# First loads in one line on SyncE, and the first block in halves: a SwiGLU feed-forward kernel on Trainium2

## The chip, the cores and the metric

The kernel runs on one core of one Trainium2 chip. The metric is the device time of one execution in microseconds, the median of several runs. Before the change it is 163.57 us (three runs, 163.53 to 163.64).

## The reference

The program computes a SwiGLU feed-forward layer on 2048 rows of 640 values, with 1536 hidden channels, all in bf16:

```python
# x (1, 2048, 640), w_gate (640, 1536), w_up (640, 1536), w_down (1536, 640)
def reference(x, w_gate, w_up, w_down):
    g = _silu(x @ w_gate)
    u = x @ w_up
    return (g * u) @ w_down
```

## The kernel before

The 2048 rows are worked in four blocks of 512 (`S_BLK`), the 1536 hidden channels in twelve f chunks of 128, and the 640 input channels in five slices of 128, which the code calls kd. For each block and each f chunk, five matmuls (one for each kd) build the gate product in a PSUM tile `pg`, and five the up product in `pu`; weights are the stationary operand, 128 x 128, and the transposed input `xT` streams 512 columns past it. ScalarE applies Silu to `pg` (L214), VectorE multiplies the result with `pu` and writes `aT` (L215). After the twelve chunks of a block, the down projection follows on TensorE: twelve matmuls into `po_t` (L261) and 48 into `po_a` (L291), which ScalarE copies out and SyncE stores.

The last four rows are computed on VectorE instead, by dot products that run beside the matmuls of the later blocks (L147); they and the late transfers for them are not touched by the change.

**How the input gets its transposed form.** The matmuls need x with its channels on the partitions. For rows 0 to 255 (`HALF`), two chunks of 128 rows are loaded as they are (L86) and turned on TensorE, five transposes each (L185); ScalarE copies the first two slices of each chunk to `xT`, VectorE the other three (L190). For all other rows the transfer engines turn the data themselves, in a crossbar copy (a transposing DMA, L105); the one for rows 256 to 511 is the first of them.

**The order of the front.** The instructions of an engine run in the order in which they are written, and a transfer is issued by an engine's queue in that order too. SyncE issues: x chunk 0, the gate slices of kd 0, 2, 3, 4 for f chunks 0 to 3 (`EARLY`, L115, 128 KB each), the crossbar copy of rows 256 to 511, the up weights of f chunks 0 to 3 in two loads (L83, 320 KB each), and then gate and up weights of chunks 4 to 7 and of chunks 8 to 11 (`W_CHUNKS`, 640 KB each), the down weights (1920 KB), and the rest. ScalarE issues x chunk 1 and the gate slice of kd 1, then loads its function table and runs a first Silu (L119). Eight semaphores serve the transfers in turn, so a load waits at its issue for the one eight before it.

TensorE starts with 18 matmuls on a constant tile (`warm`, L176, `N_WARM`), whose result is not used. Then come the ten transposes, and in `head()` the gate products of f chunks 0 to 3 together, kd by kd: kd 0 in two parts of 128 columns, kd 1 to 4 on 256 columns (the first half of the block), then all five on the second half, which needs the crossbar copy. These four `pg` tiles stay open at the same time. Then the up products of the four chunks follow on 512 columns each, and Silu and multiply for each. From f chunk 4 on the regular loop runs (L245 on), with 512 columns in every matmul. PSUM has four buffers of the tag `gu` and two each of `po_a` and `po_b`; the up tiles of the head use the latter two.

Of the kernel before, what the change touches and what calls it, by code (L numbers as in the profile page):

```python
# [10 lines left out]
def _body(  # L11
# [8 lines left out]
    nc = tc.nc  # L20
    P = nc.NUM_PARTITIONS
    f32 = mybir.dt.float32
    bf16 = mybir.dt.bfloat16
    ACT = mybir.ActivationFunctionType
    ALU = mybir.AluOpType
# [7 lines left out]
    KD = D // P  # L33
    KF = F // P
    S_BLK = 512
    NSB = S // S_BLK
    SUB = S_BLK // P
    HALF = S_BLK // 2
    DA = 512
    Q = 32  # L40
    N_WARM = 18
    T = 4
    WT_STEP = 4
    ROW_J = 0
    EARLY = 4
    W_CHUNKS = [(4, 8), (8, 12)]
    assert D % P == 0 and F % P == 0 and S % S_BLK == 0 and D > DA and SUB == 4

    consts = ctx.enter_context(tc.tile_pool(name="consts", bufs=1))
# [2 lines left out]
    psum = ctx.enter_context(  # L52
        tc.tile_pool(name="psum", bufs=2, space=bass.MemoryType.PSUM)
    )
# [3 lines left out]
    xT = consts.tile([P, KD, S], bf16)  # L58
    wg_sb = consts.tile([P, KD, F], bf16)
    wu_sb = consts.tile([P, KD, F], bf16)  # L60
    wd_sb = consts.tile([P, KF, D], bf16)
    aT = consts.tile([P, KF, S], bf16)
# [12 lines left out]
    wg_v = w_gate.rearrange("(kd p) f -> p kd f", p=P)  # L75
    wu_v = w_up.rearrange("(kd p) f -> p kd f", p=P)
    wd_v = w_down.rearrange("(kf p) d -> p kf d", p=P)

    def wslice(a, b):
        return slice(a * P, b * P)  # L80

    def load_w(eng, dst, src, a, b):
        eng.dma_start(out=dst[:, :, wslice(a, b)], in_=src[:, :, wslice(a, b)])  # L83

    def load_x(eng, c0, c1):
        eng.dma_start(out=x_sb[:, c0:c1, :], in_=x_v[:, c0:c1, :])  # L86
# [20 lines left out]
    ones = consts.tile([P, P], bf16)  # L107
    silu_first = consts.tile([P, 1], f32)
    nc.vector.memset(ones[:], 1.0)  # L109

    load_x(nc.sync, 0, 1)
    load_x(nc.scalar, 1, 2)
    for kd in range(KD):
        eng = nc.scalar if kd == 1 else nc.sync
        eng.dma_start(  # L115
            out=wg_sb[:, kd, wslice(0, EARLY)], in_=wg_v[:, kd, wslice(0, EARLY)]
        )
    turn_x(HALF, S_BLK)
    nc.scalar.activation(silu_first[:], ones[:, 0:1], ACT.Silu)  # L119
    for a in range(0, EARLY, 2):  # L120
        load_w(nc.sync, wu_sb, wu_v, a, a + 2)
    for a, b in W_CHUNKS:
        load_w(nc.sync, wg_sb, wg_v, a, b)
        load_w(nc.sync, wu_sb, wu_v, a, b)
# [4 lines left out]
    def turn_w(dst, src, f0, f1):  # L129
# [7 lines left out]
        out=x_row[:],  # L137
        in_=x2[S - T : S, :].rearrange("t d -> (t d)").partition_broadcast(P),
# [35 lines left out]
    def warm(n):  # L174
        for _ in range(n):
            nc.tensor.matmul(  # L176
                pw[:, 0:P], lhsT=ones[:], rhs=ones[:], start=True, stop=True
            )

    def transpose_chunk(c, parts):  # L180
        c_sl = slice(c * P, (c + 1) * P)
        for copy, tag, k0, k1 in parts:
            pt = psum.tile([P, k1 - k0, P], bf16, tag=tag, name="pt")
            for kd in range(k0, k1):
                nc.tensor.transpose(  # L185
                    out=pt[:, kd - k0, :],
                    in_=x_sb[:, c, kd * P : (kd + 1) * P],
                    identity=ident[:],
                )
            copy(out=xT[:, k0:k1, c_sl], in_=pt[:])  # L190

    def proj_step(ps, w_sb, fc, sb, c0, c1, kd):
        nc.tensor.matmul(  # L193
            ps[:, c0:c1],
            lhsT=w_sb[:, kd, fc * P : (fc + 1) * P],
            rhs=xT[:, kd, sb * S_BLK + c0 : sb * S_BLK + c1],
            start=(kd == 0 and c0 in (0, HALF)),
            stop=(kd == KD - 1),
        )

    def proj(ps, w_sb, fc, sb, c0, c1):
        for kd in range(KD):
            proj_step(ps, w_sb, fc, sb, c0, c1, kd)

    def gu_tiles():
        pg = psum.tile([P, S_BLK], f32, tag="gu", name="pg", bufs=4)
        pu = psum.tile([P, S_BLK], f32, tag="gu", name="pu", bufs=4)
        return pg, pu

    def gate(pg, pu, sb, fc, n_s):  # L210

        s0 = sb * S_BLK
        sg = work.tile([P, S_BLK], f32, name="sg")
        nc.scalar.activation(sg[:, 0:n_s], pg[:, 0:n_s], ACT.Silu)  # L214
        nc.vector.tensor_tensor(  # L215
            out=aT[:, fc, s0 : s0 + n_s], in0=sg[:, 0:n_s], in1=pu[:, 0:n_s], op=ALU.mult
        )

    def head():
        dve, act = nc.vector.tensor_copy, nc.scalar.copy  # L220
        split = [(act, "po_a", 0, 2), (dve, "po_b", 2, KD)]
        pgs = [
            psum.tile([P, S_BLK], f32, tag="gu", name="pg", bufs=4)
            for _ in range(EARLY)
        ]
        warm(N_WARM)
        for c in range(HALF // P):
            transpose_chunk(c, split)

        steps = [(0, 0, P), (0, P, HALF)]  # L230
        steps += [(kd, 0, HALF) for kd in range(1, KD)]
        steps += [(kd, HALF, S_BLK) for kd in range(KD)]
        for kd, c0, c1 in steps:
            for fc in range(EARLY):
                proj_step(pgs[fc], wg_sb, fc, 0, c0, c1, kd)

        for fc in range(EARLY):
            pu = psum.tile([P, S_BLK], f32, tag=("po_a", "po_b")[fc % 2], name="pu")
            proj(pu, wu_sb, fc, 0, 0, S_BLK)
            gate(pgs[fc], pu, 0, fc, S_BLK)  # L240
        keep_order(mybir.EngineType.PE)
        keep_order(mybir.EngineType.Activation)

    head()
    for sb in range(NSB):  # L245
        n_s = S_BLK if sb < NSB - 1 else S_BLK - T
        for fc in range(KF):
            if sb == 0 and fc < EARLY:
                continue
            pg, pu = gu_tiles()  # L250
            proj(pg, wg_sb, fc, sb, 0, n_s)
            proj(pu, wu_sb, fc, sb, 0, n_s)
            gate(pg, pu, sb, fc, n_s)
            if sb > 0 and fc < KF - 2:
                do_dots(2)


        n_t = (SUB if sb < NSB - 1 else SUB - 1) * P
        po_t = psum.tile([P, n_t], f32, tag="po_b", name="po_t")
        for kf in range(KF):  # L260
            nc.tensor.matmul(  # L261
                po_t[:],
                lhsT=wd_sb[:, kf, DA:D],
                rhs=aT[:, kf, sb * S_BLK : sb * S_BLK + n_t],
                start=(kf == 0),
                stop=(kf == KF - 1),
            )
        ot_t = outp.tile([P, n_t], bf16, name="ot_t")
        ot_q = outp.tile([P, n_t], bf16, name="ot_q")
        nc.scalar.copy(ot_t[:], po_t[:])  # L270
        do_dots(3)
        nc.vector.transpose(out=ot_q[:], in_=ot_t[:])  # L272
        for q in range(P // Q):
            nc.scalar.dma_start(
                out=out2[
                    sb * S_BLK : sb * S_BLK + n_t, DA + q * Q : DA + (q + 1) * Q
                ].rearrange("(i r) c -> r i c", r=Q),
                in_=ot_q[q * Q : (q + 1) * Q, :].rearrange("r (i c) -> r i c", c=Q),
            )
# [141 lines left out]
```

## Time and profile before

| what | value |
|---|---|
| median of 3 runs | 163.57 us (163.53 to 163.64) |
| profiled execution, first to last instruction | 161.8 us |
| TensorE busy | 159.4 us, 808 matmuls |
| VectorE busy | 111.0 us |
| ScalarE busy | 42.6 us |
| bytes moved by the transfer engines | 15.86 MB |
| granted TensorE clock, mean | 1.000 |

The profiled execution is told by its span, 161.8 us from the first to the last instruction; the time of a run is measured around it and is some 1.8 us longer. Its own time is not listed beside the span, so the runs' median stands for it. All start times in the profile count from the first instruction. A matmul's busy time includes the time until its result has drained, which overlaps the next matmul; what a matmul costs in a row of them is the distance from start to start.

### The profile page before, as it was taken

The page shows a single profiled execution, that of the slowest core. Times are in us where ns is not written, and L with a number is a line of the kernel's source. Part 1 is how long each engine was busy: PE and PEld are TensorE (multiplying, and loading weights), DVE is VectorE, ACT ScalarE, POOL GpSimd, SP SyncE. Part 2 cuts the span into 40 slices and gives each one's busy share as a digit, 9 for nine tenths or more (in the row PEclk, how much of TensorE's full clock was granted, in tenths as well). Part 3 has the DMA queues.
Part 4 walks back from the last instruction along what each step waited for, and adds up shares of the span by engine and source line. Part 5 has one row for each costly group of instructions (what it writes and reads, how often), then busy time and mean ns, then how long its engine had stood idle before and what let it go on. Part 6 is the DMA issues. An engine that isn't in the chain of part 4 may idle for free.

```text
span 161.8 us, 2142 instructions
## 1 busy us (share of the span) xinstructions
PE 159.4 (99%) x808; PEld 77.6 (48%) x808; DVE 111.0 (69%) x250; ACT 42.6 (26%) x74; POOL 0.6 (0%) x6
## 2 busy tenths in 40 slices
PE   8999999999999999999999999999999999999995
PEld 7854444444444444444444444444444444445454
DVE  2034223599569999989919999979964999993001
ACT  5051222112222222211222322221214222222121
POOL 1000000000000000000000000000000000000000
PEclk9999999999999999999999999999999999999999
DMA  6999999934189999003110000000321000000312
GB/s 212 231 351 349 361 248 231 222 75 91 34 192 159 235 236 184 4 0 34 65 65 0 0 4 2 0 0 3 62 67 34 0 0 0 0 0 4 48 41 73
DMA packets 41961, 15.86 MB, mean 98 GB/s; under 512 B 33504, under 2 KB 41824, under 8 KB 41952
## 3 DMA queue, kind: packets, MB, share of 16 engines
q1 hardware_dynamic: 33584, 14.93, 37.0%
q10 hardware_dynamic: 8368, 0.80, 3.5%
q8 instruction: 6, 0.10, 0.3%
q14 instruction: 3, 0.02, 0.1%
HBM read 6.88 MB, written 2.62 MB: 59 GB/s over the span
## 4 chain that ended last, share of the span: by engine, by line
PE 97%; DMA 2%; SPq 0%; DVE 0%; issue 0%
PE pg L193 32%; PE pu L193 32%; PE po_a L291 26%; PE po_t L261 6%; DMA wg_sb<-in_w_gate_dram 2%; SPq L86 0%; DVE ot_b L302 0%
## 5 line engine op out<-in xcount | busy, mean ns | idle before, releaser
L193 PE MATMUL pg<-xT,wg_sb 128*128 128x512 bf16 (+3 forms) x264 | 59.8, 363 | 0.1
L193 PE MATMUL pu<-xT,wu_sb 128*128 128x512 bf16 (+1 forms) x240 | 59.1, 379 | 0.0
L215 DVE TENSOR_TENSOR aT<-sg,pu 128x512 bf16<-128x512 f32 (+1 forms) x48 | 32.7, 682 | 32.3 <-PE pu L193 32.3
L214 ACT ACTIVATE sg<-pg 128x512 f32<-128x512 f32 (+1 forms) x48 | 28.4, 597 | 71.2 <-PE pg L193 67.4
L291 PE MATMUL po_a<-wd_sb,aT 128*128 128x512 bf16 (+4 forms) x228 | 42.8, 348 | 0.0
L147 DVE SCALAR_TENSOR_TENSOR prod<-wgT,x_row 128x640 f32<-128x640 bf16 x48 | 39.4, 821 | 1.5 <-DMA wgT<-in_w_gate_dram 0.4
L147 DVE SCALAR_TENSOR_TENSOR prod<-wuT,x_row 128x640 f32<-128x640 bf16 x48 | 39.4, 821 | 1.0
L193 PEld LDWEIGHTS <-wg_sb 128*128 128x128 bf16 x264 | 25.9, 100 | 26.8 <-DMA wg_sb<-in_w_gate_dram 0.4
L193 PEld LDWEIGHTS <-wu_sb 128*128 128x128 bf16 x240 | 23.4, 98 | 28.1 <-DMA wu_sb<-in_w_up_dram 0.3
L291 PEld LDWEIGHTS <-aT 128*128 128x128 bf16 x228 | 20.8, 98 | 21.7
L300 ACT CAST ot<-po_a 128x512 bf16<-128x512 f32 (+2 forms) x17 | 9.5, 559 | 31.8 <-PE po_a L291 20.2
L261 PE MATMUL po_t<-aT,wd_sb 128*128 128x512 bf16 (+1 forms) x48 | 10.4, 366 | 0.0
L261 PEld LDWEIGHTS <-wd_sb 128*128 128x128 bf16 x48 | 4.7, 98 | 5.1
L302 DVE CAST ot_b<-po_a 128x96 bf16<-128x96 f32 (+1 forms) x2 | 0.5, 240 | 9.7 <-PE po_a L291 9.6
L270 ACT CAST ot_t<-po_t 128x512 bf16<-128x512 f32 (+1 forms) x4 | 2.2, 559 | 11.6 <-PE po_t L261 11.6
L147 DVE DVE_READ_ACCUMULATOR prod<-wgT,x_row 128x1 f32 x48 | 3.9, 82 | 0.0
L147 DVE DVE_READ_ACCUMULATOR prod<-wuT,x_row 128x1 f32 x48 | 3.9, 82 | 0.0
L272 DVE STREAM_TRANSPOSE ot_q<-ot_t 128x512 bf16<-128x512 bf16 (+1 forms) x4 | 2.7, 676 | 1.7 <-ACT ot_t L270 1.7
L190 DVE COPY xT<-pt 128x384 bf16<-128x384 bf16 x2 | 0.7, 358 | 2.9 <-PE pt L185 2.9
L176 PE MATMUL pw<-ones 128*128 128x128 bf16 x18 | 2.1, 313 | 0.4 <-DVE ones L109 0.4
L176 PEld LDWEIGHTS <-ones 128*128 128x128 bf16 x18 | 1.8, 147 | 0.4 <-DVE ones L109 0.4
L119 ACT ACT_TABLE_LOAD x1 | 1.3, 1283 | 1.0 <-issue 1.0
(13 smaller groups left out, 4.7 us busy)
## 6 DMA issues: line engine op xcount, KB each, us to landing
wd_sb<-in_w_down_dram SPq DMA_DIRECT2D x1, 1920.0 KB, 13.0
out_dram<-ot SPq DMA_DIRECT2D x15, 128.0 KB, 1.7
wg_sb<-in_w_gate_dram SPq DMA_DIRECT2D x2, 640.0 KB, 7.9
wu_sb<-in_w_up_dram SPq DMA_DIRECT2D x2, 640.0 KB, 8.6
wu_sb<-in_w_up_dram SPq DMA_DIRECT2D x2, 320.0 KB, 4.7
x_row<-in_x_dram SPq DMA_DIRECT2D x1, 640.0 KB, 5.1
wg_sb<-in_w_gate_dram SPq DMA_DIRECT2D x4, 128.0 KB, 3.4
out_dram<-ot_q ACTq DMA_DIRECT2D x12, 32.0 KB, 1.9
```

The lines of the kernel that those rows point to most:

```text
L119: nc.scalar.activation(silu_first[:], ones[:, 0:1], ACT.Silu)
L147: nc.vector.scalar_tensor_tensor(out=prod[:], in0=wT[:, fc, :], scalar=1.0, in1=x_row[:, t, :], op0=ALU.mult, op1=ALU.mult, accum_out=acc[ ...
L176: nc.tensor.matmul(pw[:, 0:P], lhsT=ones[:], rhs=ones[:], start=True, stop=True)
L190: copy(out=xT[:, k0:k1, c_sl], in_=pt[:])
L193: nc.tensor.matmul(ps[:, c0:c1], lhsT=w_sb[:, kd, fc * P : (fc + 1) * P], rhs=xT[:, kd, sb * S_BLK + c0 : sb * S_BLK + c1], start=(kd == 0 ...
L214: nc.scalar.activation(sg[:, 0:n_s], pg[:, 0:n_s], ACT.Silu)
L215: nc.vector.tensor_tensor(out=aT[:, fc, s0 : s0 + n_s], in0=sg[:, 0:n_s], in1=pu[:, 0:n_s], op=ALU.mult)
L261: nc.tensor.matmul(po_t[:], lhsT=wd_sb[:, kf, DA:D], rhs=aT[:, kf, sb * S_BLK : sb * S_BLK + n_t], start=(kf == 0), stop=(kf == KF - 1),)
L270: nc.scalar.copy(ot_t[:], po_t[:])
L272: nc.vector.transpose(out=ot_q[:], in_=ot_t[:])
L291: nc.tensor.matmul(po[:], lhsT=aT[:, kf, s0 : s0 + P], rhs=wd_sb[:, kf, c0:c1], start=(kf == 0), stop=(kf == KF - 1),)
L300: nc.scalar.copy(ot[:], po[:])
```

## The change

The function names stay; these are the edits.

- **Loads.** SyncE issues the first loads in the order of their use: x chunk 0, gate kd 0, x chunk 1, gate kd 1, gate kd 3 and 4 in one load, up kd 0, up kd 1 and 2, up kd 3 and 4 (all for f chunks 0 to 3), then gate and up weights of f chunks 4 and 5 (`HALVED` is 6; 320 KB each), and only then the crossbar copy of rows 256 to 511. ScalarE runs the first Silu, with its table load, ahead of its only load, gate kd 2. The remaining weights come in chunks 6 to 8 and 9 to 11 (480 KB each).
- **The head.** 15 warm-up matmuls in place of 18; x chunk 0 is turned; two more warm-up matmuls (`N_GAP`); the gate products of kd 0 on columns 0 to 127; x chunk 1 is turned; then kd 1 on columns 0 to 127, and kd 0 and kd 1 on columns 128 to 255; then kd 2 to 4 on 256 columns.
- **Halves.** Gate and up products of f chunks 0 to 5 are computed on 256 columns at a time: the first half of the block for all six chunks, then the second half for all six. Gate and up share one PSUM tile (`pgu`, two halves of 256 columns). Silu and multiply run on 256 columns for these. From f chunk 6 on the regular loop takes over.

TensorE has 43 matmuls more (a warm-up matmul less, 44 others more).

```diff
-    N_WARM = 18
+    N_WARM = 15
+    N_GAP = 2
...
-    W_CHUNKS = [(4, 8), (8, 12)]
+    HALVED = 6
+    W_CHUNKS = [(6, 9), (9, 12)]
...
+    def load_d(eng, dst, src, k0, k1):
+        eng.dma_start(
+            out=dst[:, k0:k1, wslice(0, EARLY)], in_=src[:, k0:k1, wslice(0, EARLY)]
+        )
+
+    nc.scalar.activation(silu_first[:], ones[:, 0:1], ACT.Silu)
     load_x(nc.sync, 0, 1)
-    load_x(nc.scalar, 1, 2)
-    for kd in range(KD):
-        eng = nc.scalar if kd == 1 else nc.sync
-        eng.dma_start(
-            out=wg_sb[:, kd, wslice(0, EARLY)], in_=wg_v[:, kd, wslice(0, EARLY)]
-        )
+    load_d(nc.sync, wg_sb, wg_v, 0, 1)
+    load_x(nc.sync, 1, 2)
+    load_d(nc.sync, wg_sb, wg_v, 1, 2)
+    load_d(nc.scalar, wg_sb, wg_v, 2, 3)
+    load_d(nc.sync, wg_sb, wg_v, 3, KD)
+    load_d(nc.sync, wu_sb, wu_v, 0, 1)
+    load_d(nc.sync, wu_sb, wu_v, 1, 3)
+    load_d(nc.sync, wu_sb, wu_v, 3, KD)
+    load_w(nc.sync, wg_sb, wg_v, EARLY, HALVED)
+    load_w(nc.sync, wu_sb, wu_v, EARLY, HALVED)
     turn_x(HALF, S_BLK)
-    nc.scalar.activation(silu_first[:], ones[:, 0:1], ACT.Silu)
-    for a in range(0, EARLY, 2):
-        load_w(nc.sync, wu_sb, wu_v, a, a + 2)
     for a, b in W_CHUNKS:
...
         warm(N_WARM)
-        for c in range(HALF // P):
-            transpose_chunk(c, split)
-
-        steps = [(0, 0, P), (0, P, HALF)]
-        steps += [(kd, 0, HALF) for kd in range(1, KD)]
-        steps += [(kd, HALF, S_BLK) for kd in range(KD)]
-        for kd, c0, c1 in steps:
+        transpose_chunk(0, split)
+        warm(N_GAP)
+        early_gate(0, 0, P)
+        transpose_chunk(1, split)
+        for kd, c0 in ((1, 0), (0, P), (1, P)):
+            early_gate(kd, c0, c0 + P)
+        for kd in range(2, KD):
+            early_gate(kd, 0, HALF)
+        for kd in range(KD):
             for fc in range(EARLY):
-                proj_step(pgs[fc], wg_sb, fc, 0, c0, c1, kd)
-
+                proj_step(pairs[fc][:, 1, :], wu_sb, fc, 0, kd, kd == 0)
         for fc in range(EARLY):
-            pu = psum.tile([P, S_BLK], f32, tag=("po_a", "po_b")[fc % 2], name="pu")
-            proj(pu, wu_sb, fc, 0, 0, S_BLK)
-            gate(pgs[fc], pu, 0, fc, S_BLK)
+            gate(pairs[fc][:, 0, :], pairs[fc][:, 1, :], fc, 0)
+
+        halves = [(0, fc) for fc in range(EARLY, HALVED)]
+        halves += [(HALF, fc) for fc in range(HALVED)]
+        for r0, fc in halves:
+            if r0 == 0:
+                tag, bufs = ("po_a", "po_b")[fc % 2], 2
+            else:
+                tag, bufs = "gu", 4
+            pair = psum.tile([P, 2, HALF], f32, tag=tag, name="pgu", bufs=bufs)
+            proj(pair[:, 0, :], wg_sb, fc, r0)
+            proj(pair[:, 1, :], wu_sb, fc, r0)
+            gate(pair[:, 0, :], pair[:, 1, :], fc, r0)
...
-            if sb == 0 and fc < EARLY:
+            if sb == 0 and fc < HALVED:
```

`early_gate(kd, c0, c1)` issues the gate matmuls of one kd and one range of columns for f chunks 0 to 3, into the first half of each chunk's `pgu`.

More of the change, by code (lines that the diff above doesn't have):

```diff
@@ L190, in transpose_chunk, with proj_step, proj, gate @@
             copy(out=xT[:, k0:k1, c_sl], in_=pt[:])
-    def proj_step(ps, w_sb, fc, sb, c0, c1, kd):
+    def proj_step(ps, w_sb, fc, r0, kd, start):
+        n = ps.shape[-1]
         nc.tensor.matmul(
-            ps[:, c0:c1],
+            ps,
             lhsT=w_sb[:, kd, fc * P : (fc + 1) * P],
-            rhs=xT[:, kd, sb * S_BLK + c0 : sb * S_BLK + c1],
-            start=(kd == 0 and c0 in (0, HALF)),
+            rhs=xT[:, kd, r0 : r0 + n],
+            start=start,
             stop=(kd == KD - 1),
         )
-    def proj(ps, w_sb, fc, sb, c0, c1):
+    def proj(ps, w_sb, fc, r0):
         for kd in range(KD):
[L203 to L212, printed above, removed]
+            proj_step(ps, w_sb, fc, r0, kd, kd == 0)
+    def gate(pg, pu, fc, r0):
+        n = pg.shape[-1]
         sg = work.tile([P, S_BLK], f32, name="sg")
-        nc.scalar.activation(sg[:, 0:n_s], pg[:, 0:n_s], ACT.Silu)
+        nc.scalar.activation(sg[:, 0:n], pg, ACT.Silu)
         nc.vector.tensor_tensor(
-            out=aT[:, fc, s0 : s0 + n_s], in0=sg[:, 0:n_s], in1=pu[:, 0:n_s], op=ALU.mult
+            out=aT[:, fc, r0 : r0 + n], in0=sg[:, 0:n], in1=pu, op=ALU.mult
         )
@@ L221, in head, with early_gate @@
         split = [(act, "po_a", 0, 2), (dve, "po_b", 2, KD)]
-        pgs = [
-            psum.tile([P, S_BLK], f32, tag="gu", name="pg", bufs=4)
+        pairs = [
+            psum.tile([P, 2, HALF], f32, tag="gu", name="pgu", bufs=4)
             for _ in range(EARLY)
         ]
-        warm(N_WARM)
-        for c in range(HALF // P):
-            transpose_chunk(c, split)
-        steps = [(0, 0, P), (0, P, HALF)]
-        steps += [(kd, 0, HALF) for kd in range(1, KD)]
-        steps += [(kd, HALF, S_BLK) for kd in range(KD)]
-        for kd, c0, c1 in steps:
+        def early_gate(kd, c0, c1):
+            for fc in range(EARLY):
+                proj_step(
+                    pairs[fc][:, 0, c0:c1], wg_sb, fc, c0, kd, kd == 0 and c0 == 0
+                )
+        warm(N_WARM)
+        transpose_chunk(0, split)
[7 more added lines that the diff above has]
+        for kd in range(KD):
             for fc in range(EARLY):
-                proj_step(pgs[fc], wg_sb, fc, 0, c0, c1, kd)
+                proj_step(pairs[fc][:, 1, :], wu_sb, fc, 0, kd, kd == 0)
         for fc in range(EARLY):
-            pu = psum.tile([P, S_BLK], f32, tag=("po_a", "po_b")[fc % 2], name="pu")
-            proj(pu, wu_sb, fc, 0, 0, S_BLK)
-            gate(pgs[fc], pu, 0, fc, S_BLK)
+            gate(pairs[fc][:, 0, :], pairs[fc][:, 1, :], fc, 0)
[10 more added lines that the diff above has]
+            gate(pair[:, 0, :], pair[:, 1, :], fc, r0)
         keep_order(mybir.EngineType.PE)
@@ L247, in _body @@
         for fc in range(KF):
-            if sb == 0 and fc < EARLY:
+            if sb == 0 and fc < HALVED:
                 continue
[L250 to L253, printed above, removed]
+            pg = psum.tile([P, S_BLK], f32, tag="gu", name="pg", bufs=4)
+            pu = psum.tile([P, S_BLK], f32, tag="gu", name="pu", bufs=4)
+            proj(pg[:, 0:n_s], wg_sb, fc, sb * S_BLK)
+            proj(pu[:, 0:n_s], wu_sb, fc, sb * S_BLK)
+            gate(pg[:, 0:n_s], pu[:, 0:n_s], fc, sb * S_BLK)
             if sb > 0 and fc < KF - 2:
```

## The prediction

> **What bounds the kernel now.** I read the page's busy shares and chain first, then the chain in order of time, then the first 14 us engine by engine.
>
> ```profile
> PE 159.4 (99%) x808; PEld 77.6 (48%) x808; DVE 111.0 (69%) x250; ACT 42.6 (26%) x74; POOL 0.6 (0%) x6
> PE 97%; DMA 2%; SPq 0%; DVE 0%; issue 0%
> L193 PEld LDWEIGHTS <-wg_sb 128*128 128x128 bf16 x264 | 25.9, 100 | 26.8 <-DMA wg_sb<-in_w_gate_dram 0.4
> L193 PEld LDWEIGHTS <-wu_sb 128*128 128x128 bf16 x240 | 23.4, 98 | 28.1 <-DMA wu_sb<-in_w_up_dram 0.3
> ```
>
> TensorE is 97% of the chain. The waits of its weight loads on a transfer are 0.4 us (gate slices) and 0.3 us (up slices). The chain in order of time tells where its work begins:
>
> ```profile
> 0.45 3.21 DMA wg_sb<-in_w_gate_dram
> 3.71 5.21 PE pg L193 x44
> 8.92 4.37 PE pu L193 x20
> 13.29 1.08 PE pg L193 x5
> 30.55 2.59 PE po_t L261 x12
> ```
>
> From 3.71 us on it is matmuls end to end, so only the front of the program can pay. The timeline of the front (start, length, engine, line; "SPq" and "ACTq" are the issuing of transfers):
>
> ```profile
> 0.00 0.39 SPq L86 DMA_DIRECT2D x_sb<-in_x_dram  x1
> 0.13 0.38 ACTq L86 DMA_DIRECT2D x_sb<-in_x_dram  x1
> 0.39 2.10 PE L176 MATMUL pw<-ones 128*128 128x128 bf16 x18 [0.39 <-DVE ones L109]
> 0.45 1.84 SPq L115 DMA_DIRECT2D wg_sb<-in_w_gate_dram  x4
> 0.54 0.45 ACTq L115 DMA_DIRECT2D wg_sb<-in_w_gate_dram  x1
> 1.02 1.28 ACT L119 ACT_TABLE_LOAD   x1 [1.02 <-issue]
> 2.31 1.25 PE L185 MATMUL pt<-ident,x_sb 128*128 128x128 bf16 x10
> 2.32 0.20 ACT L119 ACTIVATE silu_first<-ones 128x1 f32<-128x1 bf16 x1
> 2.33 1.91 SPq L105 DMA_TRANSPOSE xT<-in_x_dram  x1
> 2.74 0.37 ACT L190 COPY xT<-pt 128x256 bf16<-128x256 bf16 x1 [0.22 <-PE pt L185]
> 4.29 1.15 SPq L83 DMA_DIRECT2D wu_sb<-in_w_up_dram  x2
> ```
>
> And TensorE's matmuls by stage (length, busy, count of those that run in the stretch; one or two of each count began before it):
>
> ```profile
> 0.39:2.31 1.92, 1.92 (x18) 1.00 0.64 188
> 3.35:3.71 0.36, 0.21 (x2) 1.00 0.65 182
> 4.54:4.96 0.42, 0.42 (x4) 1.00 1.19 211
> 4.96:6.47 1.51, 1.51 (x15) 1.00 0.87 186
> 6.57:8.75 2.18, 2.18 (x21) 1.00 0.97 291
> 13.12:30.39 17.27, 17.27 (x82) 1.00 1.11 289
> ```
>
> Three rates are in them. The 18 warm-up matmuls of 128 columns take 1.92/18 = 0.107 us each, and the two of 256 columns that start from 4.54 to 4.96 take 0.42/2 = 0.21: the array is at half rate. From 4.96 on one of 256 columns takes 2.18/20 = 0.109 and one of 512 takes 17.27/80 = 0.216. So a matmul costs by its columns, twice as much before 4.96 as after; the granted-clock column shows 1.00 throughout and hides this. What 128 columns cost at the full rate stands at the kernel's end, where twelve of 192 and twelve of 96 columns run:
>
> ```profile
> 157.92:158.91 0.99, 0.99 (x14) 1.00 0.40 132
> 158.91:159.42 0.51, 0.51 (x15) 1.00 0.00 0
> ```
>
> 0.99/12 = 0.083 and 0.51/12 = 0.043, so about 0.056 for 128 (an estimate on the line between them).
>
> **The change, part by part.** The profiled span is 161.8 us, 1.8 below the median of 163.57; I add differences to the median.
>
> *Earlier start.* Before, the array has at 4.96 finished ten transposes, eight gate matmuls of 128 columns and two of 256; two more of 256 bring it to six chunk-steps of 256 plus two, at 4.96 + 0.22 = 5.18. After, the 15 warm-up matmuls end at 0.39 + 15 x 0.107 = 1.99. x's first chunk now has no other queue's packets beside it; it lands between 1.99 and today's 2.31; I take 2.1. The five transposes take 0.53; ScalarE's copy starts 0.43 after the first of them (2.74 - 2.31) and lasts 0.37, so the gate can start some 0.84 after the landing: 2.94. The two gap matmuls (0.21) lie inside that wait and cost nothing; without them TensorE would only idle there. Then four gate matmuls (0.43), five transposes (0.53), eight gate matmuls (0.86) reach 4.76; of the last four, two run at 0.107 and two at 0.056: 5.08. That is the same place as 5.18, a gain of 0.10. Ends: 0 if x lands at 2.31 after all, 0.25 if at 1.99 and the full rate comes 0.2 sooner. This needs the first gate slice by 2.94; it lands at 3.7 today, as one of two queues' loads.
>
> *Stops that go.* From 4.96 to 8.79 before, 34 matmuls at 0.109 are 3.71 of 3.83 us; the other 0.12 (0.08 near 6.5, before the half that the crossbar copy fills, and 0.04 at the first up slice) goes.
>
> *Smaller matmuls.* From that place on, 80 of 256 columns stand where 40 of 512 stood: 80 x 0.109 - 40 x 0.216 = +0.08. Silu and multiply are cut in half with them; even at the full width they fit under the 10 x 0.109 = 1.09 us that TensorE takes for one halved f chunk:
>
> ```profile
> L215 DVE TENSOR_TENSOR aT<-sg,pu 128x512 bf16<-128x512 f32 (+1 forms) x48 | 32.7, 682 | 32.3 <-PE pu L193 32.3
> L214 ACT ACTIVATE sg<-pg 128x512 f32<-128x512 f32 (+1 forms) x48 | 28.4, 597 | 71.2 <-PE pg L193 67.4
> ```
>
> So they cost nothing, while PSUM's buffers are freed at that pace. Sum so far: -0.10 - 0.12 + 0.08 = -0.14.
>
> *Supply.* The new order needs more bytes sooner: x 320 KB, gate slices 640, up slices 640, chunks 4 and 5 of both 640: 2240 KB, 2.29 MB, all ahead of the crossbar copy; before, the first four chunks need 1600 KB of plain loads, with the crossbar copy (256 rows, 320 KB) in their midst. The transfers of the first 10 us, in 40 slices of 0.25 us, and issue to landing:
>
> ```profile
> GB/s 0 0 0 0 169 189 353 366 293 313 332 320 291 234 205 311 302 264 246 175 200 287 292 172 84 74 166 201 264 295 303 348 326 336 348 350 354 340 365 369
> DMA packets 4114, 2.46 MB, mean 246 GB/s; under 512 B 1457, under 2 KB 4114, under 8 KB 4114
> wu_sb<-in_w_up_dram SPq DMA_DIRECT2D x2, 320.0 KB, 4.7
> wg_sb<-in_w_gate_dram SPq DMA_DIRECT2D x4, 128.0 KB, 3.4
> x_sb<-in_x_dram SPq DMA_DIRECT2D x1, 160.0 KB, 2.3
> wg_sb<-in_w_gate_dram ACTq DMA_DIRECT2D x1, 128.0 KB, 3.3
> xT<-in_x_dram SPq DMA_TRANSPOSE x1, 4.2
> ```
>
> At today's pace 2.29 MB have moved by 9.5 us (2.46 MB less two slices at 0.36 MB/us). From 4.5 to 7.0 the crossbar copy and what follows it run below 290 GB/s and lose about 250 KB, 0.87 us; after, that hole comes behind these loads: 9.5 - 0.87 = 8.65. Landing comes later than the mean packet: the first 960 KB (0.98 MB) had moved by 4.5, and the last of them landed at 1.85 + 3.4 = 5.25, 0.75 later. So the up slice of chunks 4 and 5 lands at about 9.4; ends: 9.0 (all packets at 315 GB/s from 1.5 on, 0.09 MB before) and 10.25 (hole kept). TensorE wants it after 12 gate, 20 up and 5 gate matmuls: 5.08 + 37 x 0.109 = 9.11. It waits 0.3, between 0 and 1.1. Queued behind that wait is all of TensorE. The slices ahead of it are wanted with 0.2 to 0.7 us in hand on the same reckoning. ScalarE's own load, now behind 1.28 + 0.20 us of table and first Silu, is issued at about 1.65 and lands by 5.0 (3.3 later); it is wanted at 5.08.
>
> *Crossbar copy.* It follows that slice. Today it lands at 2.33 + 4.2 = 6.53, 1.3 after the last load ahead of it; then 10.7. It is wanted 15 matmuls after the late slice: 9.11 + 0.3 + 1.64 = 11.05. It costs nothing, with 0.35 in hand. The later loads (four of 480 KB instead of 640) are wanted from 17 us on and have seconds in hand.
>
> Sum: -0.14 + 0.30 = +0.16; 163.57 + 0.16 = 163.7.
>
> **Two rules weighed.** In the first 3 us, with both queues filled, the slices show 293 to 366 GB/s from 1.5 to 3.0; when ScalarE's loads are done (the last lands at 0.54 + 3.3 = 3.84), SyncE's queue alone shows 205 to 311 from 3.25 to 4.5. The Trainium skill, DMA: Bandwidth & Descriptors, section "Issuing engines are not separate DMA queues", says transfers issued by different engines run on the same 16 DMA engines and interleave, so that a second issuer only saves issue time. By that rule, one line on SyncE would keep the higher rate, the slice would land at 9.0, and the sum would be -0.14; the trace speaks rather against it.
>
> The half rate ends at 4.96, 4.57 us after the first matmul, with 0.4 us of idle in between. The Trainium skill, TensorE: Matmul & The Clock Gate, Part 1, says the array's clock is released after a busy window of about 3.4 us, and that the windows run freely. The change leaves about 0.3 us of idle in the same stretch, so by the trace the release stays where it is; by that rule it can also come another window later.
>
> **The rivals.** *Supply keeps up.* The slice lands by 9.1. For it: two slices of 0.25 us at the lower rate are all that separates 9.0 from 9.4. Then -0.14, to -0.3 with the earlier start at its far end: 163.4.
>
> *Full rate later.* A wait for the first gate slice past 2.94, or the shorter warm-up, lets the release slip. Each microsecond of slip costs half a microsecond (0.107 against 0.056): 164.0 with one, 165.1 with 3.4. Against it: the idle is no longer than before.
>
> *Supply falls behind, the other side.* The small loads keep the 205 to 260 GB/s of 3.25 to 3.75 and the slice lands at 9.9: waits of 0.8 sum to +0.66, 164.2. It decides from a wait of 0.47 on, where the sum passes +0.33.
>
> *The line gains nothing at the start.* x still lands at 2.3; the 0.10 is lost: 163.8.
>
> **How the numbers follow.** 0.2% (0.33 us) is about what a measurement of this kernel can tell from no change. Wait of 0.1 to 0.47 (forecast, with or without the gain at the start): 0.38, 163.5 to 163.9. Supply keeps up: 0.26, 163.2 to 163.5, of which 0.10 lies below 163.24. Supply falls behind: 0.25, 163.9 to 164.5. Full rate later: 0.08. Something of the front better than both ends: 0.03. So faster 0.13, same 0.54, slower 0.33. The range 163.2 to 164.4 leaves out the late release and the tails.
>
> **What would show it.** TensorE's first transposes at 2.0 to 2.2 and first gate matmul near 2.95; the 256-column spacing of 0.109 from about 4.9; no stop near 6.4; a wait of a weight load on an up slice of 0 to 0.5 us near 9.1; the first output matmul at 30.4 + 0.2 in place of 30.39. The prediction is wrong if that wait exceeds 0.5, if an earlier slice is late, or if the full rate moves by over 0.5 us.

## The result, and the profile after

| | before | after |
|---|---|---|
| median of 6 runs each, on one chip | 163.60 us (163.53 to 163.99) | 165.44 us (164.76 to 166.29) |
| ratio to before, with its 95% interval | 1 | 1.0111 [1.0083, 1.0139] |
| span of the profiled execution | 161.8 us | 164.2 us |
| first output matmul of block 0 in the chain | 30.55 us | 32.96 us |

The change costs 1.84 us. The two profiled executions are 2.4 us apart, and 32.96 - 30.55 = 2.41 of that is there when block 0's down projection begins: all of it is lost in the front. Where both are listed, a run takes 1.3 to 1.4 us more than its span in all but one case (165.54 and 164.2 for the kernel after), so the execution profiled before took about 163.1 us, an estimate, some 0.5 under its median; that is most of why the spans differ by more than the medians. Three runs, one of experiment 5 and two of experiment 7, took over 1.5% longer than the fastest of their kernel and are left out of the times and ratios. The page of the kernel after, in the rows that answer to those shown of before (busy shares, the chain by engine, the costliest groups):

```profile
PE 160.3 (98%) x840; PEld 82.3 (50%) x851; DVE 111.8 (68%) x256; ACT 43.6 (27%) x80; POOL 0.6 (0%) x6
...
PE 95%; DMA 2%; SPq 1%; issue 0%; DVE 0%
...
L203 PEld LDWEIGHTS <-wg_sb 128*128 128x128 bf16 x278 | 27.7, 103 | 27.1 <-DMA wg_sb<-in_w_gate_dram 1.5
...
L203 PEld LDWEIGHTS <-wu_sb 128*128 128x128 bf16 x270 | 26.4, 98 | 25.4
...
L220 DVE TENSOR_TENSOR aT<-sg,pgu 128x256 bf16<-128x256 f32 x12 | 4.8, 419 | 11.1 <-ACT sg L219 11.1
...
L219 ACT ACTIVATE sg<-pgu 128x256 f32<-128x256 f32 x12 | 4.4, 383 | 11.4 <-PE pgu L203 11.3
```

The wait for gate slices went from 0.4 to 1.5 us. The up slices, on which the prediction staked its wait, show no wait at all. The chain of the kernel after in order of time (start, length, what):

```profile
1.38 3.84 DMA wg_sb<-in_w_gate_dram
5.27 14.74 PE pgu L203 x124
...
32.96 2.59 PE po_t L285 x12
```

A gate slice issued at 1.38 lands at 5.22 and starts the unbroken row of matmuls at 5.27. Before, that row began at 3.71. It is kd 1, which was wanted at 3.90 by the prediction's own reckoning (2.94 + 0.43 + 0.53). The timeline of the front, kernel after:

```profile
0.00 0.39 SPq L88 DMA_DIRECT2D x_sb<-in_x_dram  x1
0.12 1.28 ACT L118 ACT_TABLE_LOAD   x1
...
0.37 0.40 ACTq L114 DMA_DIRECT2D wg_sb<-in_w_gate_dram  x1
...
0.45 0.41 SPq L114 DMA_DIRECT2D wg_sb<-in_w_gate_dram  x1
...
0.91 0.43 SPq L88 DMA_DIRECT2D x_sb<-in_x_dram  x1
1.38 0.91 SPq L114 DMA_DIRECT2D wg_sb<-in_w_gate_dram  x2
1.42 0.20 ACT L118 ACTIVATE silu_first<-ones 128x1 f32<-128x1 bf16 x1
...
2.22 0.71 PE L194 MATMUL pt<-ident,x_sb 128*128 128x128 bf16 x5
...
3.45 0.61 PE L203 MATMUL pgu<-xT,wg_sb 128*128 128x128 bf16 x4 [0.30 <-DMA wg_sb<-in_w_gate_dram]
...
3.85 0.74 PE L194 MATMUL pt<-ident,x_sb 128*128 128x128 bf16 x5
...
4.34 0.52 SPq L85 DMA_DIRECT2D wu_sb<-in_w_up_dram  x1
...
5.24 3.65 SPq L107 DMA_TRANSPOSE xT<-in_x_dram  x1
5.26 3.54 PEld L203 LDWEIGHTS <-wg_sb 128*128 128x128 bf16 x24 [0.94 <-DMA wg_sb<-in_w_gate_dram]
5.27 3.82 PE L203 MATMUL pgu<-xT,wg_sb 128*128 128x128 bf16 x24 [0.68 <-DMA wg_sb<-in_w_gate_dram]
...
8.93 2.35 PE L203 MATMUL pgu<-xT,wu_sb 128*128 128x256 bf16 x20
```

TensorE turns x chunk 0 at 2.22, as forecast. Then it stands for the first gate slice until 3.45 and for kd 1 until 5.27. Its matmuls by stage (length, busy, count that run in the stretch, granted clock, DMA share, GB/s), kernel after:

```profile
2.94:3.45 0.51, 0.21 (x3) 1.00 0.79 236
4.38:5.27 0.89, 0.21 (x3) 1.00 0.91 252
5.27:6.52 1.25, 1.25 (x12) 1.00 1.07 362
6.52:8.65 2.13, 2.13 (x12) 1.00 1.05 325
8.93:11.11 2.18, 2.18 (x22) 1.00 1.30 225
```

Twelve of 128 columns take 1.25/12 = 0.104, and the ten of 256 that start from 6.52 to 8.65 take 0.213: half rate. The twenty that start from 8.93 take 0.109. The full rate came at about 8.75, not at 4.96.

Against the forecast this closes. The up products were to start at 5.08 + 12 x 0.109 = 6.39 and start at 8.93, 2.54 late: 5.27 - 3.90 = 1.37 from the two late slices, and (8.93 - 5.27) - (6.39 - 3.90) = 1.17 from the half rate. With TensorE that late, the forecast wait of 0.30 didn't arise: 0.16 + 2.54 - 0.30 = 2.40 of the 2.41. This only says where TensorE's time went in one execution. What to charge it to needed the experiments, since the two parts can stand in for each other.

Transfers by stretch, seen from SyncE's queue (length, granted clock, DMA share, GB/s), first before, then after:

```profile
1.00:4.50 3.50, 1.00 0.91 282
3.00:4.50 1.50, 1.00 0.84 268
```

```profile
1.00:4.50 3.50, 1.00 0.83 217
3.00:4.50 1.50, 1.00 0.75 145
```

In the first 4.5 us the kernel after moves 3.5 x 217 = 0.76 MB where before moved 0.99. The missing 0.23 MB are worth 0.7 us at the 330 GB/s of later slices (an estimate). The loads weren't issued later as a whole: in both timelines the last of the first 960 KB (both x chunks, all gate slices) has been issued by 2.29 us. Single ones were: in the line x chunk 1 leaves at 0.91 in place of 0.13, and kd 1 at 1.38 in place of 0.54.

### The profile page after: what moved, and what is told of

The parts are those of the page before. It is cut to its first block, busy times and chain, and to the rows that moved or that the text cites. A ratio compares the mean times of both kernels' runs of the same rounds, so it can differ in the third digit from the quotient of the medians.

```text
span 164.2 us, 2232 instructions
## 1 busy us (share of the span) xinstructions
PE 160.3 (98%) x840; PEld 82.3 (50%) x851; DVE 111.8 (68%) x256; ACT 43.6 (27%) x80; POOL 0.6 (0%) x6
## 4 chain that ended last, share of the span: by engine, by line
PE 95%; DMA 2%; SPq 1%; issue 0%; DVE 0%
PE pu L203 28%; PE pg L203 27%; PE po_a L315 26%; PE pgu L203 9%; PE po_t L285 6%; DMA wg_sb<-in_w_gate_dram 2%; SPq L88 1%; SPq L114 0%; DVE ot_b L326 0%
## 5 line engine op out<-in xcount | busy, mean ns | idle before, releaser
L203 PE MATMUL pu<-xT,wu_sb 128*128 128x512 bf16 (+1 forms) x210 | 52.1, 379 | 0.0
L203 PE MATMUL pg<-xT,wg_sb 128*128 128x512 bf16 (+1 forms) x203 | 51.7, 379 | 0.4
L220 DVE TENSOR_TENSOR aT<-sg,pu 128x512 bf16<-128x512 f32 (+1 forms) x42 | 28.7, 683 | 22.2 <-PE pu L203 22.2
L203 PEld LDWEIGHTS <-wg_sb 128*128 128x128 bf16 x278 | 27.7, 103 | 27.1 <-DMA wg_sb<-in_w_gate_dram 1.5
L219 ACT ACTIVATE sg<-pg 128x512 f32<-128x512 f32 (+1 forms) x42 | 25.0, 596 | 60.2 <-PE pg L203 57.1
L203 PEld LDWEIGHTS <-wu_sb 128*128 128x128 bf16 x270 | 26.4, 98 | 25.4
L220 DVE TENSOR_TENSOR aT<-sg,pgu 128x256 bf16<-128x256 f32 x12 | 4.8, 419 | 11.1 <-ACT sg L219 11.1
L203 PE MATMUL pgu<-xT,wg_sb 128*128 128x256 bf16 (+1 forms) x68 | 10.1, 304 | 1.0 <-DMA wg_sb<-in_w_gate_dram 1.0
L203 PE MATMUL pgu<-xT,wu_sb 128*128 128x256 bf16 x60 | 8.0, 273 | 0.0
L219 ACT ACTIVATE sg<-pgu 128x256 f32<-128x256 f32 x12 | 4.4, 383 | 11.4 <-PE pgu L203 11.3
```

Source lines behind the costliest of these rows:

```text
L203: nc.tensor.matmul(ps, lhsT=w_sb[:, kd, fc * P : (fc + 1) * P], rhs=xT[:, kd, r0 : r0 + n], start=start, stop=(kd == KD - 1),)
L219: nc.scalar.activation(sg[:, 0:n], pg, ACT.Silu)
L220: nc.vector.tensor_tensor(out=aT[:, fc, r0 : r0 + n], in0=sg[:, 0:n], in1=pu, op=ALU.mult)
```

## The experiments

Two explanations stood at the start: the idle of TensorE puts off the full rate, and this is the loss; or the loads come late, whatever the rate. All ratios are to the kernel before on the same chip, with 95% intervals.

### 1. Idle filled, loads untouched

```diff
-    N_WARM = 15
-    N_GAP = 2
+    N_WARM = 17
+    N_GAP = 6
+    N_FILL = 8
...
         transpose_chunk(1, split)
+        for _ in range(N_FILL):
+            nc.tensor.matmul(
+                pairs[3][:, 1, 0:P], lhsT=ones[:], rhs=ones[:], start=False, stop=False
+            )
```

The added matmuls write where the up product starts over; they are extra work, and no load is touched.

> The changed kernel, loads untouched, with TensorE's idle pieces of the front filled by more unused matmuls: 17 in place of 15 at the start, 6 in place of 2 in the gap, and 8 ahead of the gate matmuls of kd 1. Theory A (the full rate came 3.8 us later than before, at 8.8 in place of 4.96, because the array idled 1.65 us between 2.0 and 5.3; that is most of the loss): the full rate comes at 4.5 to 5.5 and the time is 163.6 to 164.2. Theory B (the full rate falls where it falls, and the late loads are the loss): still near 8.8, 165.0 to 165.8.

Measured: 165.44 us, 1.0114 [1.0091, 1.0137], the same as the change. The full rate is there at 3.2 us. The waits of the weight loads (total, times, longest):

```profile
PEld L204 <- DMA xT<-in_x_dram: 1.1, 1, 1.1
PEld L204 <- DMA wg_sb<-in_w_gate_dram: 0.9, 1, 0.9
PEld L204 <- DMA wu_sb<-in_w_up_dram: 0.3, 1, 0.3
```

In the profiled execution the early rate is lost again in waits, the longest for the crossbar copy, which lands only at 12.93. That wait is not one of supply: the copy's last packet had moved by 10.88, and its landing came 2.05 us later, where the other 16 profiles show 0.46 to 0.62. So the profile doesn't tell why the other three runs (165.18 to 165.97) are no faster. What the experiment shows is that filling the idle gains nothing in the median.

### 2. Two queues as before

```diff
-    nc.scalar.activation(silu_first[:], ones[:, 0:1], ACT.Silu)
     load_x(nc.sync, 0, 1)
+    load_x(nc.scalar, 1, 2)
     load_d(nc.sync, wg_sb, wg_v, 0, 1)
-    load_x(nc.sync, 1, 2)
-    load_d(nc.sync, wg_sb, wg_v, 1, 2)
-    load_d(nc.scalar, wg_sb, wg_v, 2, 3)
+    load_d(nc.scalar, wg_sb, wg_v, 1, 2)
+    load_d(nc.sync, wg_sb, wg_v, 2, 3)
     load_d(nc.sync, wg_sb, wg_v, 3, KD)
+    nc.scalar.activation(silu_first[:], ones[:, 0:1], ACT.Silu)
```

> The changed kernel with the first loads on two queues again: x chunk 1 and gate kd 1 on ScalarE ahead of the table load, gate kd 0, 2, 3-4 on SyncE; everything else as changed. Theory A with the load order as the cause of the idling: gate kd 0 and 1 land by 3.9, idle under 0.6 us in all, full rate near 5, 163.3 to 163.8. If the late loads have another cause (the finer order of the head wants them too soon): waits for gate slices of 0.5 us and more stay, 164.5 and above.

Measured: 164.36 us, 1.0038 [1.0019, 1.0058]: two thirds of the loss are gone, with everything else of the change in place. The same stretches seen from SyncE's queue:

```profile
1.00:4.50 3.50, 1.00 0.95 274
3.00:4.50 1.50, 1.00 0.91 265
```

kd 1 lands at 3.72 in place of 5.22. The up slice of chunks 4 and 5 still lands at 10.19. With two engines issuing, it also leaves sooner, at 3.89 in place of 4.34; in experiment 5 the later loads leave no later than before.

### 3. The kernel before with a short warm-up

```diff
-    N_WARM = 18
+    N_WARM = 9
```

> The kernel before with 9 warm-up matmuls in place of 18, nothing else: TensorE idles 0.96 us more, from 1.35 to 2.31, and no load moves. Theory A: the full rate comes later than 4.96, up to one window, and the time is 164.4 to 165.4. Theory B: full rate near 4.96, 163.5 to 163.8.

Measured: 163.85 us, 1.0015 [0.9996, 1.0034]. In the profile TensorE is idle for 0.9 us more and the full rate comes at 6.4 in place of 4.96; the first output matmul starts at 30.92, 0.53 later than before (30.39 by its start; the chain shows it 0.16 later). A late full rate can cost something, but here the median can't tell it from nothing.

### 4. All first loads on SyncE

```diff
-    load_d(nc.scalar, wg_sb, wg_v, 2, 3)
+    load_d(nc.sync, wg_sb, wg_v, 2, 3)
```

> The changed kernel with gate kd 2 on SyncE too, after gate kd 1, so that ScalarE issues no load at the front. Theory C (ScalarE's load, issued at 0.37 and landing at 3.19, runs ahead of gate kd 0 and pushes the line back): gate kd 0 lands by 3.0 in place of 3.4 and gate kd 1 by 4.7 in place of 5.2, the full rate is still late, 164.6 to 165.4. Rival (the line itself reads slowly, 74 to 177 GB/s from 3.25 to 4.25): gate kd 1 still at 5.0 or later, 165.2 to 166.0.

Measured: 165.03 us, 1.0078 [1.0058, 1.0098]. kd 0 lands at 2.69 and kd 1 at 4.25, in place of 3.40 and 5.22, so the first slices are better. But the supply as a whole is not: 238 GB/s from 1.0 to 4.5, the up slice of chunks 4 and 5 at 11.13, the crossbar copy at 12.26, and 0.8 us of waits for up slices.

### 5. The line alone, in the kernel before

```diff
-    load_x(nc.sync, 0, 1)
-    load_x(nc.scalar, 1, 2)
-    for kd in range(KD):
-        eng = nc.scalar if kd == 1 else nc.sync
...
     nc.scalar.activation(silu_first[:], ones[:, 0:1], ACT.Silu)
+    load_x(nc.sync, 0, 1)
+    load_d(nc.sync, 0, 1)
+    load_x(nc.sync, 1, 2)
+    load_d(nc.sync, 1, 2)
+    load_d(nc.scalar, 2, 3)
+    load_d(nc.sync, 3, KD)
+    turn_x(HALF, S_BLK)
```

> The kernel before with the first part of the change alone: x and gate slices in one line on SyncE (kd 2 on ScalarE, its table load ahead), crossbar copy still straight after them, no halves, 18 warm-up matmuls. Theory D (the line itself makes gate kd 1 land past 5 and opens the idle pieces): x chunk 1 lands near 3.7 and gate kd 1 near 5.2, the full rate comes past 6, 164.2 to 165.2. Rival (the line costs only together with the finer head and the deeper queue behind it): 163.4 to 163.8.

Measured: 164.85 us (163.85 to 165.76), 1.0076 [1.0046, 1.0105]. The line alone, without halves and without loads ahead of the crossbar copy, costs most of what the whole change costs. Its profile is of its fastest run, 163.85, and even that shows x chunk 1 landing at 3.65 and kd 1 at 5.28. Its transfers, seen from SyncE's queue:

```profile
1.00:4.50 3.50, 1.00 0.80 227
3.00:4.50 1.50, 1.00 0.68 170
```

The later loads leave no later than before: the crossbar copy at 2.34 against 2.33, the first up load at 3.96 against 4.29. From 3.0 us on, with the first 960 KB issued by 2.29 in both kernels, 170 GB/s stand against 268, so the lower rate there is not a matter of issue time.

### 6. Two queues and four halved chunks

Experiment 2, with chunks 4 and 5 back in the regular loop and behind the crossbar copy:

```diff
-    HALVED = 6
-    W_CHUNKS = [(6, 9), (9, 12)]
+    HALVED = 4
+    W_CHUNKS = [(4, 8), (8, 12)]
...
-    load_w(nc.sync, wg_sb, wg_v, EARLY, HALVED)
-    load_w(nc.sync, wu_sb, wu_v, EARLY, HALVED)
```

> The kernel of the two-queue run with four f chunks halved in place of six: the 640 KB of chunks 4 and 5 go behind the crossbar copy again. Theory E (with two queues the rest of the loss is supply: the up slice of chunk 5 lands at 10.2 where 9.1 is wanted): no wait for chunks 4 and 5, the crossbar copy lands at 9.0 to 9.8 and is wanted at 9.2, 163.6 to 164.1. If the 0.8 us that the two-queue run loses come from the front (waits for gate slices up to 6.3): unchanged, 164.2 to 164.6.

Measured: 164.34 us, 1.0064 [1.0034, 1.0094]. It is inconclusive: TensorE stands for 0.60 us until 9.92, when no load is late (the copy lands at 9.07). The second half of the first chunks then asks for the `gu` buffers, which the first half still holds; the profile names VectorE's multiply as what ends the wait. That is a wait of the edit's own making; experiment 10 removes it.

### 7. An up load on ScalarE's queue, in the kernel before

```diff
-    for a in range(0, EARLY, 2):
-        load_w(nc.sync, wu_sb, wu_v, a, a + 2)
+    load_w(nc.sync, wu_sb, wu_v, 2, EARLY)
...
             transpose_chunk(c, split)
+        load_w(nc.scalar, wu_sb, wu_v, 0, 2)
+        warm(3)
```

> The kernel before with two additions: three unused matmuls between the transposes and the first gate matmul (the 0.36 us of idle), and the first up load (320 KB) issued by ScalarE after its two copies, beside the crossbar copy, in place of behind it on SyncE. If idle sets when the full rate comes and the up load sets what an earlier rate can gain: full rate before 4.5, first up load lands at 7 to 7.8 in place of 8.75, 162.9 to 163.4. If the load beside them delays the gate slices or the crossbar copy: 163.6 to 164.2.

The three unused matmuls fill TensorE's idle ahead of the first gate slice. Measured: 164.08 us (163.76 to 165.34), 1.0044 [1.0017, 1.0071]. The load, now issued behind ScalarE's copies, left at 4.26, where before it left at 4.29; it landed at 9.37 in place of 8.75, and TensorE waited 0.5 us for it. A second queue is no gain by itself; it has to carry the load early.

### 8. Two queues, idle filled

Experiment 2 with `N_WARM` 18, `N_GAP` 6 and two unused matmuls at the place of experiment 1.

> The kernel of the two-queue run with TensorE's idle pieces filled (18 warm-up matmuls, 6 in the gap, 2 ahead of kd 1). Theory E (supply): the full rate comes before 4.5, and what it gives is lost again in waits for the up slice of chunk 5 and the crossbar copy: 164.1 to 164.5, as without the fill. If the late full rate were the loss: 163.3 to 163.8.

Measured: 164.39 us, 1.0051 [1.0027, 1.0075]. Full rate at 3.94 in place of 4.7, and no gain over experiment 2 that can be told: its profile still shows waits of 0.7 us for gate and 0.4 for up slices, where experiment 2 has 0.8 and 0.4.

### 9. kd 1 and kd 2 change queues

```diff
-    load_d(nc.sync, wg_sb, wg_v, 1, 2)
-    load_d(nc.scalar, wg_sb, wg_v, 2, 3)
+    load_d(nc.sync, wg_sb, wg_v, 2, 3)
+    load_d(nc.scalar, wg_sb, wg_v, 1, 2)
```

> The changed kernel with two gate slices exchanged between the queues: kd 1 on ScalarE (issued at 0.37), kd 2 on SyncE in its place in the line. Theory F (the loss of the line is that the slice wanted next, gate kd 1, sits fourth in it and lands at 5.2): kd 1 lands near 3.2, the wait of 0.9 us ahead of it goes, kd 2 lands near 5.2 and costs 0.3 to 0.5, 164.3 to 164.9. Rival (the reading of the line as a whole is slow and every later load carries the delay): the waits only move to later loads, 165.1 to 165.7.

Measured: 165.0 us, 1.0100 [1.0065, 1.0136]. kd 1 is no longer late, but x chunk 1 lands at 4.12 and kd 2 at 5.03; 171 GB/s from 3.0 to 4.5, full rate at 8.8. So it isn't one unlucky slice: either of the two comes late from that place of the line while ScalarE's load runs beside it. Without that load (4, and 14 below) kd 1 lands at 4.25 from the same place.

### 10. Experiment 6 without its wait for PSUM

```diff
-            if r0 == 0:
+            if fc < 2:
                 tag, bufs = ("po_a", "po_b")[fc % 2], 2
```

> The kernel with two queues and four f chunks halved, its second half beginning in the PSUM buffers of po_a and po_b, so that it need not wait for Silu and multiply of the first (0.66 us at 9.9 in the run before it). Theory E (chunks 4 and 5 ahead of the crossbar copy cost the two-queue kernel its 0.8 us): 163.5 to 163.9. Rival (the front's gate slices cost it): 164.1 to 164.5.

Measured: 163.27 us where before has 163.31, 1.0009 [0.9986, 1.0033]. The crossbar copy lands at 8.84, and after 3.57 us TensorE waits for nothing. From the chain in order of time:

```profile
30.69 2.59 PE po_t L283 x12
```

That is 0.14 from before's 30.55. The split head, the merged gate and up tile and the half-width Silu and multiply cost nothing that can be measured.

### 11. A second profile of both kernels

One run of each, with a profile and unaltered.

> The changed kernel once more, for a second profile. If windows of fixed length run freely and the first one that TensorE fills to some three quarters sets the full rate, it comes somewhere from 3.2 to 9 us, by the phase, and not at 8.8 again but by chance; the rate of the transfers from 3 to 4.5 us falls below 200 GB/s again if that belongs to the line. If the idle pieces alone set it: 8.5 to 9 again.

> The kernel before once more, for a second profile. With free windows the full rate comes anywhere from 3.2 to 6.6 us; if the 0.4 us of idle set it, 4.9 to 5.0 again. Transfers from 3 to 4.5 us at 250 GB/s or more in either case.

Measured: 164.68 us for after, 163.05 for before. After, the full rate is reached by 4.6 this time, some 4.2 us sooner than in the first profile. Its matmuls by stage, and its waits:

```profile
5.24:6.00 0.76, 0.76 (x14) 1.00 1.06 372
6.00:8.30 2.30, 2.30 (x24) 1.00 1.00 301
```

```profile
PEld L194 <- DMA x_sb<-in_x_dram: 1.3, 2, 0.9
PEld L203 <- DMA wg_sb<-in_w_gate_dram: 1.0, 3, 0.3
PEld L203 <- DMA wu_sb<-in_w_up_dram: 0.8, 2, 0.6
```

The 21 matmuls of 256 columns that start from 6.00 take 0.109 each. Now there is a wait for up slices, 0.8 us, as the prediction said there might be. The first output matmul is at 31.84, 0.96 before the first profile's 32.80 and still 1.45 behind before: with the full rate in time, the waits for loads alone cost that. The second profile of before has its full rate at 3.9 in place of 4.96, stands for 0.46 at the crossbar copy, and its first output matmul is at 30.32 against 30.39. A microsecond of full rate gave 0.07.

### 12. A longer warm-up on experiment 10

```diff
-    N_WARM = 15
-    N_GAP = 2
+    N_WARM = 20
+    N_GAP = 4
```

> Two queues, four halved chunks, second half beginning in po_a and po_b, with 20 warm-up matmuls in place of 15 and 4 in the gap in place of 2. If the supply now leaves slack and only the phase of the full rate costs: the full rate comes earlier on average, 162.9 to 163.3, 0 to 0.4 below the kernel before. If the gate slices (the last lands at 5.7 to 6.3) take the gain: 163.2 to 163.6, no difference.

Measured: 163.50 us, 1.0012 [0.9994, 1.0030]. TensorE waits for no load, and the time is that of before. The longer warm-up gained nothing, but it didn't bring the full rate sooner either: it comes at 5.82, with next to no idle ahead of it, against 5.0 in experiment 10. None of these versions beats the kernel before.

### 13. The line with four halved chunks

Experiment 10 with the line of the change in place of the two queues.

> The changed kernel with four halved chunks in place of six (chunks 4 and 5 behind the crossbar copy, second half beginning in po_a and po_b); the line on SyncE stays. If the line's loss stands by itself: 0.8 to 1.3 above the kernel before, as the line alone. If the line costs only because chunks 4 and 5 queue behind it: 0 to 0.4 above.

Measured: 165.34 us, 1.0104 [1.0069, 1.0139], with x chunk 1 at 3.93, kd 1 at 5.08 and 171 GB/s from 3.0 to 4.5. Under the line no difference can be told between chunks 4 and 5 ahead of the crossbar copy and behind it.

### 14. The line on SyncE alone, in smaller loads

```diff
-    load_d(nc.scalar, wg_sb, wg_v, 2, 3)
-    load_d(nc.sync, wg_sb, wg_v, 3, KD)
+    load_d(nc.sync, wg_sb, wg_v, 2, 3)
+    load_d(nc.sync, wg_sb, wg_v, 3, 4)
+    load_d(nc.sync, wg_sb, wg_v, 4, KD)
```

> The changed kernel with every first load on SyncE, one gate slice each (kd 3 and 4 split, no load from ScalarE). If the joint load or ScalarE's early load makes the line slow: 0.9 MB or more by 4.5 us and 164.0 to 164.6. If it is the line itself: 0.75 to 0.85 MB by 4.5 us and 164.8 to 165.4.

Measured: 164.98 us, 1.0104 [1.0088, 1.0120]. Transfers seen from SyncE's queue, and the longest wait:

```profile
1.00:4.50 3.50, 1.00 0.91 253
3.00:4.50 1.50, 1.00 0.90 246
```

```profile
PEld L204 <- DMA wu_sb<-in_w_up_dram: 2.0, 4, 0.5
```

Without ScalarE's load the hole of 140 to 171 GB/s is gone, but the up slice of chunks 4 and 5 lands at 11.06 and TensorE waits 2.0 us for up slices. Part of that can be issue time: with two loads more ahead of it on SyncE, this slice leaves at 5.26 in place of 4.34. So neither the joint load of kd 3 and 4 nor the single load on ScalarE is the sole cause. The full rate is there by 4.2 in this profile, so none of the loss in it is a late rate.

## Why the prediction was wrong

The four cells of the design, as ratio to before:

| | six halved, chunks 4 and 5 ahead of the copy | four halved, behind the copy |
|---|---|---|
| line on SyncE | 1.0111 [1.0083, 1.0139] (the change) | 1.0104 [1.0069, 1.0139] (13) |
| two queues | 1.0038 [1.0019, 1.0058] (2) | 1.0009 [0.9986, 1.0033] (10) |

The right column also has the PSUM edit of experiment 10, without which it has a wait of its own (6). The line costs 0.7 to 1.0% in either column, and 0.76% on the kernel before by itself (5). Chunks 4 and 5 ahead of the crossbar copy point to another 0.3% with two queues, though those two intervals overlap a little; under the line no further cost can be told. The halves cost nothing that can be measured with four halved chunks.

By the prediction's steps:

- **Earlier start, -0.10: failed.** x chunk 0 and its transposes came as forecast (2.22 for 2.1). The step "needs the first gate slice by 2.94" did not hold: it landed at 3.40. This condition was named, but the next slice, kd 1, had no condition of its own beyond "0.2 to 0.7 us in hand" for the slices ahead; it was 1.3 us late (5.22 for 3.90). These two are the 1.37 us of the first profile. The rows shown would have told it: a 128 KB load on SyncE took 3.4 us from issue to landing, and 1.38 + 3.4 = 4.78 is 0.9 past 3.90. The prediction used these 3.4 us for the last gate load, not for kd 1.
- **Supply, +0.30: the failing term of the sum.** The prediction took the line to move bytes at the pace of the kernel before. The transfers of the first 10 us, kernel after, in 40 slices of 0.25 us:

```profile
GB/s 0 0 0 0 189 338 176 75 270 364 384 364 240 177 107 74 106 168 217 250 303 365 365 356 369 369 332 303 295 299 326 334 346 344 344 321 296 263 180 96
DMA packets 3508, 2.43 MB, mean 243 GB/s; under 512 B 692, under 2 KB 3508, under 8 KB 3508
...
wu_sb<-in_w_up_dram SPq DMA_DIRECT2D x1, 320.0 KB, 6.0
```

  From 3.25 to 4.5 stand 177, 107, 74, 106, 168 where before had 234, 205, 311, 302, 264. The 2.29 MB have moved by 9.25 (2.43 less the last three slices, 0.13), not by 8.65, and the up slice lands 1.06 behind its mean packet, not 0.75: 4.34 + 6.0 = 10.3, not 9.4. The near end given, 9.0, doesn't follow from its own figures: 1.5 + (2.29 - 0.09)/0.315 + 0.75 is 9.2. The far end, 10.25, was nearly met, but it was read as a wait at one place, while the same shortage had already struck at kd 0 and kd 1. The rival "supply falls behind" had the mechanism and the side right; its place and its size (+0.66 for a landing at 9.9) were too small.
- **The two queues against one line.** The trace's lower rates behind 3.25 were read as "rather against" an even rate, but no price was put on it beyond the range's end. Every profile with two queues moved 260 to 289 GB/s from 1.0 to 4.5 us, and every one with the line 212 to 253. The Trainium skill, DMA: Bandwidth & Descriptors, section "Issuing engines are not separate DMA queues", would have a second issuer save issue time only; the runs differ from it: in experiment 5 the later loads leave no later than before, yet 227 GB/s move in place of 282, and the time is 0.76% longer. The 0.7% between experiment 2 and the change holds some 0.45 us of issue time as well.
- **Full rate where it was: wrong in the first profile, and a part of the loss at most.** It came at 8.75 there and by 4.6 in the second profile. The Trainium skill, TensorE: Matmul & The Clock Gate, Part 1, allows for this with windows of about 3.4 us that run freely; the traces agree in that it differs between two executions of one kernel (4.96 and 3.9 before, too). The idle ahead of it doesn't order it: 1.5 us in the second profile of the change, next to none in experiment 12, where it came at 5.82. The price of half a microsecond for each, as the rival "full rate later" had it, holds only where the loads are in time: between the two profiles of the change 4.2 us of it gave 0.96, and filling the idle (1, 8) gave nothing in the median. The loss stands without it (1.45 us in the second profile, and experiment 14), so that the rival's 165.1 lies near 165.44 is mostly luck. But a full rate past 8 us shows in three of the eight profiles with the line (the change, 9, 13) and in none of the nine with two queues; what it adds to the median is open. The sign given for it, a move of over 0.5 us, could tell nothing: the kernel before itself moved by 1.06 between its two profiles.
- **Smaller matmuls, +0.08, Silu and multiply hidden, gap matmuls free: right.** Spacing 0.109 at the full rate, 383 and 419 ns for the halves under 1.09 us of TensorE, and experiment 10 at before's time. The estimate of 0.056 for 128 columns was met: in the second profile's trace they start 0.056 apart from 4.65 on.
- **Crossbar copy costs nothing: right for the change** (it landed at 11.34, with TensorE late), though 0.6 later than the 10.7 given. The wait of 1.1 in experiment 1 came from a late landing in that one execution.
- **ScalarE's load issued at 1.65: wrong, and not shown to be free.** It went out at 0.37 and landed at 3.19, in time for itself, but ahead of kd 0 and kd 1. In experiment 4, where it follows kd 1 on SyncE, kd 0 landed 0.71 and kd 1 0.97 sooner. So much of the lateness of the first slices goes with this load; most of the time doesn't (165.03 against 165.44), since the up slices then come later.

What stays open is why the line is read slowly. Neither the slice that stands there (9), nor the single load on ScalarE or the joint load (14), nor the number of halved chunks (13) is it alone. The order of packets within the transfer engines was not tried by itself.

## What to carry to other kernels

Put the first small loads on two issuing engines, and price a move to one queue by the bytes by time, slice by slice, not by the mean rate of both. Even that can be too high: the slices in which SyncE's queue ran alone before had 205 to 311 GB/s, those of the line 74 to 177. Check each load of a reordered front against the moment its data is wanted, by its own issue time and the latency that the rows show, the first ones above all: slack of some tenths in a front that moves 0.2 MB less is none. Before a late full rate or an idle engine is blamed, fill the idle, and profile more than one execution: the moment of the full rate, and in experiment 1 a landing, were matters of one execution.

## What the runs showed of the hardware

- With one of the first loads on ScalarE (128 KB) and the rest on SyncE, fewer bytes moved early than with two on ScalarE (288 KB), though the same 960 KB were issued by 2.29 us in both: 217 against 282 GB/s from 1.0 to 4.5 us, and 145 against 268 from 3.0 to 4.5.
- ScalarE's transfer went out at 0.37, while its table load ran (0.12 to 1.40), although the Silu that needs the table (1.42) is written ahead of it.
- The moment of TensorE's full rate differs between executions of one kernel (before 4.96 and 3.9, after 8.75 and at most 4.6); over all profiles of this case it lay between 3.2 and 9.1.
- The issue of the crossbar copy held SyncE's queue for 3.65 us behind the longer line, against 1.91 before, and the next load left at 8.94. Nothing here waited for that. The issue began right after kd 1 had landed (5.24 and 5.22; 5.32 and 5.30 in experiment 1), as the eight semaphores have it.
- The crossbar copy landed 0.46 to 0.62 us after its last packet in 16 profiles, and 2.05 us after it in one (experiment 1).
